# Merging w3's load into one transfer and moving it ahead of w1 at the start of an attention-plus-MLP decode kernel

## The chip, the cores and the metric

The kernel runs on one core of one Trainium2 chip. The metric is device time in microseconds (us) of one execution. All times compared here are of the fast state, unless a run is called slow. Times inside a trace are counted from the start of the span, and the span (213.7 us before) is about 1.3 us shorter than the device time of the same run.

## The reference, cut to what matters

Four sequences, one new position each. After a layer norm, an attention branch A reads 2,048 cached keys and values for each of 4 x 16 heads, and an MLP branch B runs through four weight matrices. The sum of both goes out.

```python
xn = _layernorm(x)
return x + A(xn, k_cache, v_cache, wq, wo) + B(xn, w1, w2, w3, w4)

def B(x, w1, w2, w3, w4):            # x is (4, 1, 576): S = 1
    h = _gelu(_layernorm(x) @ w1)
    # each quarter of h is shifted by one or two positions, with zeros shifted in:
    g0 = jnp.pad(h[:, :, 0*c:1*c], ((0,0),(1,0),(0,0)))[:, :S, :]      # ... g1, g2, g3 alike
    hs = jnp.concatenate([g0, g1, g2, g3], axis=-1) @ w2
    x1 = x + hs
    return x1 + _gelu(_layernorm(x1) @ w3) @ w4    # w3 is 576 x 4608
```

## The kernel before

A list of operations with keys is sorted for each engine. All large loads are issued by SyncE onto one DMA queue, in order of key: weights first, then 16 K chunks of 2 MB, then 16 V chunks (the first half of the output weights wo among them), then the rest of the output weights.

```python
ev_wq  = [add_dma([(kt_t[:], A_wq[0:512, :]...)], "wq", (), -60),
          add_dma(rag_pair(ragq3, B_w3, A_wq), "wqr", ["ragq3_zero"], -59)]   # the last 64 rows of w3 and wq
ev_r12 = add_dma(rag_pair(rag12, B_w1, B_w2), "r12", (), -58.5)
ev_w2  = add_dma([(w2main, B_w2[0:512, :]...)], "w2", (), -58)
ev_w1  = add_dma([(w1main, B_w1[0:512, :]...)], "w1", (), -57)
w3_src = B_w3[0:512, :].rearrange("(p r) n -> p r n", r=4)
ev_w3  = [add_dma([(..., w3_src[:, 2 * h:2 * h + 2, :])], ("w3", h), (), -56 + 2 * h) for h in range(2)]
ev_w3.append(ev_wq[1])
...
for c in range(NC):      # K chunks into a ring of NPOS = 4 slots: the fifth waits for PE
    add_dma(kv_pairs(A_k_cache, c), ("k", c % NPOS), [t_done(c - NPOS)] if c >= NPOS else [], c)
```

The fifth K chunk can be issued only when PE has transposed the first one. Ahead of its K loop, PE runs the front part:

```python
add("pe", pe_zero, waits=["zeros_bf", "perm_bf", "gelu_h", "x1", "xnT"], sig=None, key=-7.5)   # clears 4 banks
add("pe", pe_h(h), waits=[ev_w1, ev_r12, "xn2T", "xnT"], sig=f"hT{h}", key=-24 + 0.1 * h)      # w1's product
for n, r in enumerate((0, 1, 4, 2, 3)):                                                        # h2 = norm(x1) @ w3
    add("pe", pe_h2(r), waits=[ev_w3[r // 2]] + ([...] if r == 0 else []), ..., key=-9 + n)
...                                                                                            # GELU, 9 transposes
for c in range(NC):                                                                            # the K loop
    for k in range(NBLK):
        w = [take(("k", c % NPOS), 16)] if k == 0 else []                                      # waits for the chunk
        add("pe", pe_T(NBLK * c + k), waits=w + [...], ..., loop=lp)
```

Of the kernel before, what the change touches and what calls it, by code (L numbers as in the profile page):

```python
# [35 lines left out]
def bass_parallel_sum__sliding_block_cached__mixer_s_mlp__decode_kernel(  # L36
# [5 lines left out]
    F = B_w3.shape[1]  # L42
# [17 lines left out]
    with ExitStack() as ctx:  # L60
        def sb(name, shape, dt):
            return ctx.enter_context(nc.sbuf_tensor(name, shape, dt))
# [6 lines left out]
        w3_t = sb("w3", [128, 4 * F], BF16)  # L69
# [15 lines left out]
        w1main = w4_t[:, 0:4 * D].rearrange("p (r n) -> p r n", r=4)  # L85
# [14 lines left out]
        xnT = sb("xnT", [128, 5, 32], BF16)  # L100
        xn2T = sb("xn2T", [128, 5, B], BF16)
        x1nT = sb("x1nT", [128, 5, 32], BF16)
# [9 lines left out]
        perm_bf = sb("perm_bf", [128, 128], BF16)  # L112
# [6 lines left out]
        zeros_bf = sb("zeros_bf", [128, 512], BF16)  # L119
# [36 lines left out]
        def add(engine, emit, waits=(), sig=None, key=0.0, inc=(), loop=None, cond=None):  # L156
            seqc[0] += 1
            prog[engine].append(Op(emit, waits, sig, key, seqc[0], inc, loop, cond))

        def tok(nm):  # L160
            if nm not in S:
                S[nm] = sem("t_" + "_".join(str(k) for k in (nm if isinstance(nm, tuple) else (nm,))))
            return nm
# [6 lines left out]
        def add_dma(pairs, skey, waits=(), key=0.0, engine="sp"):  # L170
            tok(skey)
            dma_count[skey] = dma_count.get(skey, 0) + 16 * len(pairs)

            def emit(e):
                for o_, i_ in pairs:
                    e.dma_start(o_, i_).then_inc(S[skey], 16)  # L176
            add(engine, emit, waits, None, key)
            return ("dma", skey, dma_count[skey])

        def rag_pair(tile, even, odd):  # L180
            return [(tile[p:128:2, 0:w.shape[1]], w[512:576, :]) for p, w in enumerate((even, odd))]
# [8 lines left out]
        def pool_ident(t, tag, pattern, view, key):  # L190
# [20 lines left out]
            waits=["ident_f"], sig="mU", key=-8)  # L211
        for x in range(2):
# [4 lines left out]
        ev_wq = [add_dma([(kt_t[:], A_wq[0:512, :].rearrange("(p r) n -> p (r n)", r=4))], "wq", (), -60),  # L217
                 add_dma(rag_pair(ragq3, B_w3, A_wq), "wqr", ["ragq3_zero"], -59)]
        ev_r12 = add_dma(rag_pair(rag12, B_w1, B_w2), "r12", (), -58.5)
        ev_w2 = add_dma([(w2main, B_w2[0:512, :].rearrange("(p r) n -> p r n", r=4))], "w2", (), -58)  # L220
        ev_w1 = add_dma([(w1main, B_w1[0:512, :].rearrange("(p r) n -> p r n", r=4))], "w1", (), -57)
        w3_src = B_w3[0:512, :].rearrange("(p r) n -> p r n", r=4)
        ev_w3 = [add_dma([(w3_t[:, 2 * h * F:2 * (h + 1) * F].rearrange("p (r n) -> p r n", r=2), w3_src[:, 2 * h:2 * h + 2, :])], ("w3", h), (), -56 + 2 * h)
                 for h in range(2)]
        ev_w3.append(ev_wq[1])

        def kv_pairs(cache, c):
            b, gq = CH[c]
# [84 lines left out]
        for b in range(B):  # L313
            add("dve", lambda e, b=b: e.tensor_copy(out=qp_out[:, b], in_=qp_in[:, b]), waits=["qTp", "qpad_zero"],
                sig="qT" if b == B - 1 else None, key=-29.4)
# [3 lines left out]
        def pe_zero(e):  # L319
# [1 line left out]
            for q in range(4):  # L321
                ins = e.matmul(Sps[:, q, :], lhsT=zeros_bf[:, 0:128], rhs=zeros_bf[:, :], start=True, stop=True)
            return ins
        add("pe", pe_zero, waits=["zeros_bf", "perm_bf", "gelu_h", "x1", "xnT"], sig=None, key=-7.5)
        add("act", lambda e: e.activation(out=act_dummy[:], in_=zeros_bf[0:1, 0:2], func=ACTF.Sqrt), waits=["zeros_bf"], sig="sqrt_table", key=-110)
        add("act", lambda e: e.activation(out=act_dummy[:], in_=zeros_bf[0:1, 0:2], func=ACTF.Copy), waits=["zeros_bf"], inc=[(tok("evA"), 1)], key=-0.5)
        add("dve", lambda e: e.tensor_copy(out=dve_dummy[:], in_=zeros_bf[0:1, 0:2]), waits=["zeros_bf"], inc=[(tok("evD"), 1)], key=-0.5)
# [12 lines left out]
        def evac(n):  # L340
            if n % 8 in ACT_EVAC:
                return "act", lambda e: e.activation(out=ktbuf[:, n % 16], in_=tb[n % 4], func=ACTF.Copy)  # L342
            return "dve", lambda e: e.tensor_copy(out=ktbuf[:, n % 16], in_=tb[n % 4])  # L343
# [14 lines left out]
        for c in range(NC):  # L358
            lp = ("K", c // NPOS)
            for k in range(NBLK):  # L360
# [4 lines left out]
                eng, f = evac(NBLK * c + k)  # L365
                add(eng, f, waits=[f"T{NBLK * c + k}"] + ([f"SC{c - 2}"] if c >= 2 else []), inc=[("evA" if eng == "act" else "evD", 1)],
                    key=NBLK * c + k + 0.2)
# [4 lines left out]
              waits=["qT", "qs_zero"] + ([f"SC{c - NPOS}"] if c >= NPOS - 1 else []), inc=[("qs", 1)], key=c)  # L372
# [6 lines left out]
            waits=["rmax"], sig="negb", key=KS + 0.05)  # L379
        for q in range(4):  # L380
            add("act", lambda e, q=q: e.activation(out=P_sb[:, q, :], in_=Sps[:, q, :], func=ACTF.Exp,
                                                   bias=negb[:, 0:1], scale=scale, accum_out=rs4[:, q:q + 1]),
                waits=["negb"], sig=f"exp{q}", key=KS + 0.1 + 0.01 * q)

        for q in range(4):
# [3 lines left out]
                waits=[f"PTx{q}", "permT_bf"] + (["PT0"] if q == 3 else []), sig=f"PTy{q}", key=k0)  # L389
            add("act", lambda e, q=q: e.activation(out=PT_t[:, 512 * q:512 * (q + 1)], in_=ps[:, 4 + q % 3, :], func=ACTF.Copy),  # L390
                waits=[f"PTy{q}"], sig=f"PT{q}", key=k0 + 0.16)
# [3 lines left out]
            waits=["rinv", "ident_f"], sig="diag", key=KS + 0.82)  # L395
        add("pe", lambda e: e.matmul(rinvps, lhsT=ones_f[:], rhs=diag[:], start=True, stop=True), waits=["diag", "ones_f", "exp3"],
            sig="rinvp", key=KS + 0.9)
        add("dve", lambda e: e.tensor_copy(out=rinvB[:].rearrange("p (c u e) -> p c u e", u=NU, e=2),
                                           in_=rinvps.rearrange("p (u c e) -> p c u e", u=NU, e=2)),
            waits=["rinvp"], sig="rinvB", key=KS + 1.5)  # L400
# [20 lines left out]
        for c in range(NC):  # L421
# [4 lines left out]
                key=KV + 2 * c, loop=("V", gq))  # L426
            if b == B - 1:
                hv = lambda t, gq=gq: t[:, 0:128].rearrange("p (b h) -> p b h", b=B)[:, :, 8 * gq:8 * gq + 8]
                add("dve", lambda e, hv=hv: e.tensor_tensor(out=hv(OTn), in0=OTps.rearrange("p (b h) -> p b h", b=B), in1=hv(rinvB), op=ALU.mult),  # L429
                    waits=["rinvB", f"PV{c}"], sig=f"OTn{gq}" if gq == 3 else None, inc=[(tok("otn"), 1)] if gq < 3 else [], key=KV + 2 * c + 0.1)  # L430
# [13 lines left out]
        def pe_AO(half):  # L444
# [10 lines left out]
            waits=["OTy"], sig="ORp", key=KT - 2.5)  # L455
# [15 lines left out]
        def pe_h(h):  # L471
            def f(e):
                for r in range(4):
                    e.matmul(HTps[h], lhsT=xn2T[:, r, :], rhs=w1main[:, r, HALF * h:HALF * (h + 1)], start=(r == 0), stop=False)
                return e.matmul(HTps[h], lhsT=xn2T[:, 4, :], rhs=rag12[:, HALF * h:HALF * (h + 1)], start=False, stop=True)
            return f
        for h in range(2):
            add("pe", pe_h(h), waits=[ev_w1, ev_r12, "xn2T", "xnT"], sig=f"hT{h}", key=-24 + 0.1 * h)

        def pe_hs(h):  # L480
            def f(e):
# [4 lines left out]
        for h in range(2):  # L486
# [3 lines left out]
                waits=[f"hs{h}", "ln1"], sig="x1" if h else "x1a", key=-29 + 0.6 * h)  # L490
# [3 lines left out]
        add("dve", lambda e: e.tensor_copy(out=x1nT[:, :, 0:B], in_=XTps[2]), waits=["x1T", "x1nT_zero"], sig="x1nT", key=-23)  # L494
        for h in range(2):
            add("act", lambda e, h=h: e.activation(out=h_sb[:, HALF * h:HALF * (h + 1)], in_=HTps[h], func=ACTF.Gelu_apprx_tanh),
                waits=[f"hT{h}", "x1nT"], sig="gelu_h" if h else None, key=-20 + 0.1 * h)

        segs = []
        for g in range(4):  # L500
            t = 9 * g
            while t < 9 * g + 9:
                n = next(m for m, (a, z) in enumerate(W4N) if a <= t < z)
# [4 lines left out]
        def pe_h2(r):  # L508
            def f(e):
                ins = None  # L510
                for k in range(3):
                    for g, off, cnt, base_, rc, rr in sorted(segs, key=lambda x: (x[1], x[0])):
                        w, x_ = (w3r[r], x1nT[:, r, :]) if r < 4 else (ragq3, x1nT[:, 4, :])
                        ins = e.matmul(H2ps[k][32 * g:32 * g + 32, :].rearrange("p (x c) -> p x c", c=9)[:, :, off:off + cnt], lhsT=x_,
                                       rhs=w[:, base_:base_ + 128 * rc].rearrange("p (x s) -> p x s", s=rc)[:, XS[k]:XS[k + 1], rr:rr + cnt],
                                       start=(r == 0 and off == 0), stop=(r == 3), tile_position=(0, 32 * g), skip_group_check=True)
                return ins
            return f
        for n, r in enumerate((0, 1, 4, 2, 3)):
            add("pe", pe_h2(r), waits=[ev_w3[r // 2]] + (["x1nT", "qT", "qs0", "qs1"] if r == 0 else []), sig=None if r == 2 else f"h2_{r}",  # L520
                inc=[(tok("otn"), 1)] if r == 2 else [], key=-9 + n)
        for k in range(3):
            add("act", lambda e, k=k: e.activation(out=h2g[:, 9 * XS[k]:9 * XS[k + 1]], in_=H2ps[k], func=ACTF.Gelu_apprx_tanh), waits=["h2_3"],
                sig="gelu2" if k == 2 else None, key=-0.9 + 0.1 * k)

        def pe_h2T(e):
# [7 lines left out]
            waits=["h2T"], inc=[("evA", 1)], key=-0.3)  # L534
        add("dve", lambda e: e.tensor_copy(out=h2o[:, :, 8, :], in_=H2Tb.rearrange("p (g y) -> p g y", g=4)[..., 0:B]),
            waits=["h2T"], inc=[("evD", 1)], key=-0.3)
# [112 lines left out]
```

## Time and profile before

| | before |
|---|---|
| device time, median (3 runs) | 215.03 us (214.92 to 215.20) |
| bytes read from HBM | 88.49 MB |
| DMA engines busy, 12 to 176 us | 1.00 to 1.01 |
| PE ready for K / first K chunk landed | about 34 us / 35.98 us |

These are lines of the page of before. The rows with 40 digits cut the span into 40 equal slices (5.3 us each); PEclk is the TensorE clock that was granted, in tenths of full speed, and DMA the busy share of the 16 DMA engines in tenths.

```profile
span 213.7 us, 5906 instructions
...
PEclk9999999799999999999999655555555555555799
DMA  7999999999999999999999999999999999999993
GB/s 282 406 385 449 438 411 442 414 429 422 432 426 429 429 423 435 422 432 420 439 423 432 420 425 427 427 426 435 426 423 426 429 429 426 429 429 436 426 404 124
DMA packets 6690, 88.65 MB, mean 415 GB/s; under 512 B 780, under 2 KB 1048, under 8 KB 1560
...
q1 hardware_dynamic: 6664, 88.50, 97.7%
...
DMA w<-in_B_w_dram 15%; SPq L176 1%; PE ps L417 1%; PE ps L434 1%; DVE out_sb L551 0%
```

The DMA row is full from the second slice to the last but one, and the queue q1 alone has packets in flight for 97.7% of the span. The last line is the chain that ended last: it is the transfer of w4 at the end of that queue.

The table by stretches of before (start:end in us, length, busy us of each engine, granted clock, DMA share, GB/s):

```profile
core 0: us, PE busy (x) PEld busy (x) DVE busy (x) ACT busy (x) POOL busy (x), PEclk, DMA share, GB/s
12.00:18.50 6.50, 4.29 (x45) 1.68 (x45) 1.78 (x7) 0.20 (x1) 0.00 (x0) 1.00 1.01 415
18.50:24.40 5.90, 4.40 (x26) 2.24 (x23) 2.75 (x10) 0.60 (x1) 0.76 (x3) 1.00 1.00 431
24.40:30.00 5.60, 3.93 (x67) 2.60 (x69) 2.54 (x11) 2.17 (x4) 0.00 (x0) 1.00 1.00 427
30.00:36.00 6.00, 2.48 (x57) 2.04 (x49) 0.17 (x1) 1.59 (x5) 0.00 (x0) 1.00 1.01 426
36.00:114.00 78.00, 77.21 (x1274) 63.43 (x1275) 51.42 (x79) 47.14 (x47) 3.81 (x13) 0.98 1.01 427
```

In the front part, where the change works, the DMA engines are already full. PE is only partly busy, so its waits there are waits of an engine that does not set the time. In the K loop PE is busy for 77.2 of 78 us, which looks like a second bound, but the DMA engines are full there too: the two run nearly level.

PE's timeline of before around the end of the front part (start, length, instruction, and in brackets the idle time before it and what ended it):

```profile
26.61 1.51 PE L514 MATMUL ps<-w,x1nT 128*32 128x387 bf16 x36 [0.35 <-DVE x1nT L494]
28.82 0.81 PE L322 MATMUL ps<-zeros_bf 128*128 128x512 bf16 x3 [0.70 <-ACT h_sb L496]
29.56 2.17 PE L514 MATMUL ps<-w,x1nT 128*32 128x387 bf16 x54
33.07 0.76 PE L529 MATMUL ps<-ident_bf,PT 128*128 128x128 bf16 x9 [1.35 <-ACT PT L523]
36.27 2.89 PE L336 MATMUL ps<-perm_bf,ring 128*128 128x128 bf16 x32 [2.44 <-PEq L575]
```

L514 is h2, L322 the clearing of the banks, L529 the transposes of h2, L336 the K loop. PE is idle for 2.44 us ahead of the K loop; the first K chunk's semaphore is complete at 35.98 us, so this wait is for the DMA queue.

### The profile page before, as it was taken

The page shows a single profiled execution, that of the slowest core. Times are in us where ns is not written, and L with a number is a line of the kernel's source. Part 1 is how long each engine was busy: PE and PEld are TensorE (multiplying, and loading weights), DVE is VectorE, ACT ScalarE, POOL GpSimd, SP SyncE. Part 2 cuts the span into 40 slices and gives each one's busy share as a digit, 9 for nine tenths or more (in the row PEclk, how much of TensorE's full clock was granted, in tenths as well). Part 3 has the DMA queues.
Part 4 walks back from the last instruction along what each step waited for, and adds up shares of the span by engine and source line. Part 5 has one row for each costly group of instructions (what it writes and reads, how often), then busy time and mean ns, then how long its engine had stood idle before and what let it go on. Part 6 is the DMA issues. An engine that isn't in the chain of part 4 may idle for free. (4 is left out here: it accounts for less than half of the span.)

```text
span 213.7 us, 5906 instructions
## 1 busy us (share of the span) xinstructions
PE 141.4 (66%) x2664; PEld 110.4 (52%) x2668; DVE 75.3 (35%) x147; ACT 61.2 (29%) x76; POOL 10.8 (5%) x38
## 2 busy tenths in 40 slices
PE   0038683999999999999996277133444433336995
PEld 0023363788878887888774067033434433334542
DVE  0142511477776676666664830100010001001000
ACT  2001032366655666666656620000000000000000
POOL 8300100000001000000000000000000000000000
PEclk9999999799999999999999655555555555555799
DMA  7999999999999999999999999999999999999993
GB/s 282 406 385 449 438 411 442 414 429 422 432 426 429 429 423 435 422 432 420 439 423 432 420 425 427 427 426 435 426 423 426 429 429 426 429 429 436 426 404 124
DMA packets 6690, 88.65 MB, mean 415 GB/s; under 512 B 780, under 2 KB 1048, under 8 KB 1560
## 3 DMA queue, kind: packets, MB, share of 16 engines
q1 hardware_dynamic: 6664, 88.50, 97.7%
q8 instruction: 8, 0.13, 0.2%
q14 instruction: 2, 0.02, 0.0%
q10 hardware_dynamic: 16, 0.01, 0.0%
HBM read 88.49 MB, written 0.00 MB: 414 GB/s over the span
## 5 line engine op out<-in xcount | busy, mean ns | idle before, releaser
L336 PE MATMUL ps<-perm_bf,ring 128*128 128x128 bf16 x1024 | 62.5, 221 | 3.0 <-PEq L575 2.4
L336 PEld LDWEIGHTS ps<-perm_bf,ring 128*128 128x128 bf16 x1024 | 58.3, 98 | 11.3 <-issue 11.1
L343 DVE COPY kt<-ps 128x1024 bf16<-128x1024 bf16 x80 | 52.4, 688 | 28.5 <-PE ps L336 28.0
L342 ACT ACTIVATE kt<-ps 128x1024 bf16<-128x1024 bf16 x48 | 48.4, 1023 | 33.0 <-PE ps L336 32.3
L417 PE MATMUL ps<-PTpad,ring 128*128 128x8 bf16 x1024 | 29.7, 168 | 41.5 <-PEq L575 37.5
L417 PEld LDWEIGHTS ps<-PTpad,ring 128*128 128x128 bf16 x1024 | 28.7, 104 | 42.6 <-issue 42.5
L552 ACT ACTIVATE out_sb<-ps 4x288 bf16<-4x288 f32 x1 | 0.4, 401 | 87.5 <-PE ps L434 87.5
L350 PE MATMUL ps<-kt,Qs 128*32 128x512 bf16 x272 | 18.5, 393 | 1.4 <-PEq L575 1.4
L406 DVE TENSOR_TENSOR PTpad<-PT,mU_bf 128x512 bf16<-128x512 bf16 x16 | 6.4, 421 | 29.7 <-PE ps L417 29.7
L429 DVE TENSOR_TENSOR OTn<-ps,rinvB 128x32 bf16<-128x32 f32 x4 | 0.8, 192 | 34.5 <-PE ps L417 34.5
L277 PE MATMUL ps<-ident_bf,xn_bf 4*128 4x4 bf16 x8 | 0.5, 170 | 13.9 <-DVE ragsrc L271 13.9
L350 PEld LDWEIGHTS ps<-kt,Qs 128*32 128x32 bf16 x272 | 5.9, 98 | 7.2 <-issue 2.2
L371 POOL COPY Qs<-Qpad 128x128 bf16<-128x128 bf16 x16 | 4.6, 293 | 86.8 <-PE ps L350 72.5
L277 PEld LDWEIGHTS ps<-ident_bf,xn_bf 4*128 4x128 bf16 x8 | 0.4, 111 | 14.0 <-issue 11.6
L434 PE MATMUL ps<-w,ORT 128*4 128x288 bf16 x64 | 5.8, 358 | 0.4 <-DVE ORT L456 0.4
L551 DVE CAST out_sb<-ps 4x288 bf16<-4x288 f32 x1 | 0.4, 446 | 14.5 <-PE ps L434 14.5
L434 PE MATMUL ps<-w,h2T_sb 128*4 128x288 bf16 x72 | 5.0, 286 | 0.4 <-DMA w<-in_B_w_dram 0.4
L264 ACT ACTIVATE sd<-mv 4x1 f32<-4x1 f32 x3 | 0.6, 202 | 15.8 <-DVE mv L262 15.8
L388 PE MATMUL ps<-kt,permT_bf 128*128 128x512 bf16 x3 | 1.8, 608 | 4.9 <-DVE kt L387 4.8
L434 PEld LDWEIGHTS ps<-w,ORT 128*4 128x4 bf16 x64 | 3.4, 106 | 3.0 <-DVE ORT L456 1.0
L434 PEld LDWEIGHTS ps<-w,h2T_sb 128*4 128x4 bf16 x72 | 2.9, 84 | 2.8 <-DMA w<-in_B_w_dram 1.8
L440 PE MATMUL ps<-zeros_bf 128*128 128x512 bf16 x13 | 3.8, 419 | 0.4 <-DVE OTn L429 0.2
(99 smaller groups left out, 65.9 us busy)
## 6 DMA issues: line engine op xcount, KB each, us to landing
ring<-in_A_k_cache_dram SPq DMA_DIRECT2D x16, 2048.0 KB, 14.4
ring<-in_A_v_cache_dram SPq DMA_DIRECT2D x16, 2048.0 KB, 17.4
w<-in_B_w_dram SPq DMA_DIRECT2D x2, 2304.0 KB, 21.9
w<-in_A_wo_dram SPq DMA_DIRECT2D x2, 2304.0 KB, 21.1
kt<-in_A_wq_dram SPq DMA_DIRECT2D x1, 4096.0 KB, 12.3
w<-in_B_w_dram SPq DMA_DIRECT2D x1, 2592.0 KB, 28.1
w<-in_B_w_dram SPq DMA_DIRECT2D x3, 576.0 KB, 13.6
w<-in_B_w_dram SPq DMA_DIRECT2D x1, 1296.0 KB, 30.7
```

What stands on the lines that cost most here:

```text
L277: e.transpose(XTps[idx][:, r, :], v[:, r, :], ident_bf[0:B, 0:B])
L336: ins = e.transpose(tb[n % 4][:, t, :], slot_t(c)[:, 8 * k + t, :], perm_bf[:])
L342: return "act", lambda e: e.activation(out=ktbuf[:, n % 16], in_=tb[n % 4], func=ACTF.Copy)
L343: return "dve", lambda e: e.tensor_copy(out=ktbuf[:, n % 16], in_=tb[n % 4])
L350: ins = e.matmul(Sps[32 * u:32 * u + 32, q, :].rearrange("p (t i) -> p t i", t=16), lhsT=Qs[:, c % NPOS, 32 * u:32 * u + 32], rhs=ktgrp[:, ...
L371: P(lambda e, c=c, cc=cc: e.tensor_copy(out=Qs[:, c % NPOS, :], in_=Qpad_t[:, 128 * cc:128 * cc + 128]), waits=["qT", "qs_zero"] + ([f"SC{ ...
L388: add("pe", lambda e, q=q: e.matmul(ps[:, 4 + q % 3, :], lhsT=permT_bf[:], rhs=PTx[:, q, :], start=True, stop=True), waits=[f"PTx{q}", "pe ...
L406: return lambda e: e.tensor_tensor(out=PTpad[:, c % 2], in0=PTv[:, :, cc, :].unsqueeze(2).to_broadcast([128, NT, NU, 2]), in1=mU_bf[:].uns ...
L417: ins = e.matmul(o_, lhsT=slot_t(c)[:, t, :], rhs=PTpad[:, c % 2, t].rearrange("p u e -> p (u e)"), start=(t == 0), stop=(t == NT - 1))
L429: add("dve", lambda e, hv=hv: e.tensor_tensor(out=hv(OTn), in0=OTps.rearrange("p (b h) -> p b h", b=B), in1=hv(rinvB), op=ALU.mult), waits ...
L434: return e.matmul(ACC[h], lhsT=lhsT, rhs=rhs, start=start, stop=stop, tile_position=(0, 32 * h), skip_group_check=True)
L440: ins = e.matmul(ps[:, 3, :], lhsT=zeros_bf[:, 0:128], rhs=zeros_bf[:, :], start=True, stop=True)
```

## The change

The intent: w3's 512 main rows come as one transfer, in one run of 36,864 B per partition in place of two of 18,432 B, and earlier; w1, whose result is needed later, comes behind it, and PE multiplies with w1 after h2.

```diff
-        ev_w1 = add_dma([(w1main, B_w1[0:512, :].rearrange("(p r) n -> p r n", r=4))], "w1", (), -57)
-        w3_src = B_w3[0:512, :].rearrange("(p r) n -> p r n", r=4)
-        ev_w3 = [add_dma([(..., w3_src[:, 2 * h:2 * h + 2, :])], ("w3", h), (), -56 + 2 * h) for h in range(2)]
-        ev_w3.append(ev_wq[1])
+        ev_w3 = add_dma([(w3_t[:], B_w3[0:512, :].rearrange("(p r) n -> p (r n)", r=4))], "w3", (), -57)
+        ev_w1 = add_dma([(w1main, B_w1[0:512, :].rearrange("(p r) n -> p r n", r=4))], "w1", (), -56)
...
-        add("pe", pe_zero, ..., key=-7.5)
+        add("pe", pe_zero, ..., key=-0.5)
...
-            add("pe", pe_h(h), waits=[ev_w1, ev_r12, "xn2T", "xnT"], sig=f"hT{h}", key=-24 + 0.1 * h)
+            add("pe", pe_h(h), waits=[ev_w1, ev_r12, "xn2T", "xnT"], sig=f"hT{h}", key=-3 + 0.1 * h)
...   (the GELU of h moves from key -20 to -0.69, behind that of h2)
-        for n, r in enumerate((0, 1, 4, 2, 3)):
-            add("pe", pe_h2(r), waits=[ev_w3[r // 2]] + (["x1nT", "qT", "qs0", "qs1"] if r == 0 else []), ...
+        for n, r in enumerate((4, 0, 1, 2, 3)):
+            add("pe", pe_h2(r), waits=["x1nT", "qT", "qs0", "qs1", ev_wq[1]] if r == 4 else [ev_w3], ...
```

(The accumulation's `start` flag moves with the order, from r == 0 to r == 4, the ragged 64 rows.)

More of the change, by code (lines that the diff above doesn't have):

```diff
@@ L220, in bass_parallel_sum__sliding_block_cached__mixer_s_mlp__decode_kernel @@
         ev_w2 = add_dma([(w2main, B_w2[0:512, :].rearrange("(p r) n -> p r n", r=4))], "w2", (), -58)
-        ev_w1 = add_dma([(w1main, B_w1[0:512, :].rearrange("(p r) n -> p r n", r=4))], "w1", (), -57)
-        w3_src = B_w3[0:512, :].rearrange("(p r) n -> p r n", r=4)
-        ev_w3 = [add_dma([(w3_t[:, 2 * h * F:2 * (h + 1) * F].rearrange("p (r n) -> p r n", r=2), w3_src[:, 2 * h:2 * h + 2, :])], ("w3", h), (), -56 + 2 * h)
-                 for h in range(2)]
-        ev_w3.append(ev_wq[1])
+        ev_w3 = add_dma([(w3_t[:], B_w3[0:512, :].rearrange("(p r) n -> p (r n)", r=4))], "w3", (), -57)
+        ev_w1 = add_dma([(w1main, B_w1[0:512, :].rearrange("(p r) n -> p r n", r=4))], "w1", (), -56)
         def kv_pairs(cache, c):
@@ L323, in pe_zero @@
             return ins
-        add("pe", pe_zero, waits=["zeros_bf", "perm_bf", "gelu_h", "x1", "xnT"], sig=None, key=-7.5)
+        add("pe", pe_zero, waits=["zeros_bf", "perm_bf", "gelu_h", "x1", "xnT"], sig=None, key=-0.5)
         add("act", lambda e: e.activation(out=act_dummy[:], in_=zeros_bf[0:1, 0:2], func=ACTF.Sqrt), waits=["zeros_bf"], sig="sqrt_table", key=-110)
@@ L496, in bass_parallel_sum__sliding_block_cached__mixer_s_mlp__decode_kernel @@
             add("act", lambda e, h=h: e.activation(out=h_sb[:, HALF * h:HALF * (h + 1)], in_=HTps[h], func=ACTF.Gelu_apprx_tanh),
-                waits=[f"hT{h}", "x1nT"], sig="gelu_h" if h else None, key=-20 + 0.1 * h)
+                waits=[f"hT{h}", "x1nT"], sig="gelu_h" if h else None, key=-0.69 + 0.01 * h)
         segs = []
@@ L515, in f @@
                                        rhs=w[:, base_:base_ + 128 * rc].rearrange("p (x s) -> p x s", s=rc)[:, XS[k]:XS[k + 1], rr:rr + cnt],
-                                       start=(r == 0 and off == 0), stop=(r == 3), tile_position=(0, 32 * g), skip_group_check=True)
+                                       start=(r == 4 and off == 0), stop=(r == 3), tile_position=(0, 32 * g), skip_group_check=True)
                 return ins
             return f
-        for n, r in enumerate((0, 1, 4, 2, 3)):
-            add("pe", pe_h2(r), waits=[ev_w3[r // 2]] + (["x1nT", "qT", "qs0", "qs1"] if r == 0 else []), sig=None if r == 2 else f"h2_{r}",
+        for n, r in enumerate((4, 0, 1, 2, 3)):
+            add("pe", pe_h2(r), waits=["x1nT", "qT", "qs0", "qs1", ev_wq[1]] if r == 4 else [ev_w3], sig=None if r == 2 else f"h2_{r}",
                 inc=[(tok("otn"), 1)] if r == 2 else [], key=-9 + n)
```

## The prediction

> **What bounds the kernel now.** The DMA queue. The stretch table gives a DMA share of 1.00 to 1.01 in every stretch from 12 to 176 us, at 415 to 431 GB/s; the queue table gives that queue 97.7% of the span. The idle time is the start (first packet ends about 3 us in) and the tail (last landing about 211.5 us, span 213.7 us). The chain of waits ends with 32.3 us of W4 transfer. The Trainium skill, "DMA: Bandwidth & Descriptors", section "Where 436 GB/s comes from", puts the fabric ceiling at 435 GB/s; this trace, at up to 431 GB/s, agrees. Only fewer bytes, better packets, or an idle gap can change the time.
>
> **What the change does to DMA.** Same bytes, same order up to w2, then w3 before w1. 256 packets of 18,432 B (median 686 ns each, 26.9 B/ns per engine) become 128 of 36,864 B. The packet records give 309 ns for 8,192 B and 1,222 ns for 32,768 B: about 5 ns per packet that does not scale with bytes (estimate from these two). An engine saves 8 packets, so about 0.04 us. One issue of 0.44 us leaves SyncE, which runs far ahead. Value: nothing.
>
> **What it does to PE and ACT.** Landings before (DMA semaphore records): w2 17.5, w1 18.9, w3 24.4 and 29.9, first K chunk 36.0 us. After: w3 whole at about 28.5, w1 at 29.9, first K chunk unchanged at 36.0. The layer-norm path gives x1nT at 26.5 us. h2 now does the ragged rows at 26.6 to 27.4, waits for w3 until about 28.5, then runs 72 matmuls at about 41 ns each (timeline: 54 in 2.17 us), so it ends at about 31.6 us, against 31.7 us before. The first half's early work was never the bound: the second half landed at 29.9. After it: GELU 1.3 us on ACT, with its 1.28 us table load already moved ahead of the wait (instruction order), w1's product 1.2 us on PE under it, 9 transposes 0.8 us, the second GELU 0.7 us, the zeroing matmuls about 0.8 us, now last. PE is ready for K at about 34.7 to 35 us; the first K chunk lands at 36.0, and the timeline of before shows PE idle 2.44 us for it. Roughly 1 us of slack is left; if it were overrun, PE takes about 4.7 us per K chunk against 4.9 us of transfer, and the ring's fifth issue (42.7 us) comes 8 us before the fourth chunk lands (50.7 us). None of this is on the critical path.
>
> **Predicted time: 215.0 us, 80% range 214.5 to 215.6 us. Faster by over 2%: 0.005; within 2%: 0.98; slower by over 2%: 0.015.**
>
> **What would show it.** Right: the first K chunk lands at 36.0 ± 0.2 us; PE's idle before its first transpose is still ended by that landing; 128 packets of 36,864 B at about 1,370 ns; DMA share about 1.0 from 12 to 176 us; last W4 landing about 211.5 us. h2 ends 31 to 32 us.
>
> **What would make it wrong.** The 36 KB run being cut into many short packets with a lower rate (no packet in the trace exceeds 32,768 B): 1,152 B packets run at 22.6 B/ns, which would cost w3 about 2 us. Or one DMA engine lagging through the long packets so all later landings wait on it. Or PE's wait on w3 growing past the K slack and the ring's slack together, over 8 us.

## More of the kernel before

With S = 1 every shift by one position leaves zeros only, so `hs` is zero and `h` reaches no output. The kernel before uses the zeros (`hs_inT` is a memset) but still loads w1 and w2 and runs their products.

## The result, and the profile after

| | before | after |
|---|---|---|
| device time, median (6 runs each) | 215.06 us (214.81 to 215.25) | 214.90 us (214.80 to 215.03) |
| ratio after / before | | 0.9994, 95% interval 0.9981 to 1.0007 |

A ratio here is the mean time of one kernel's fast runs over that of the other's fast runs of the same rounds, so it is not quite the ratio of the medians quoted. The time is the same.

The same lines of the page of after:

```profile
span 213.6 us, 5903 instructions
...
PEclk9999959999999999999999555555555555555799
DMA  7999989999999999999999999999999999999993
...
DMA packets 6546, 88.65 MB, mean 415 GB/s; under 512 B 764, under 2 KB 1032, under 8 KB 1544
...
q1 hardware_dynamic: 6520, 88.50, 97.8%
...
DMA w<-in_B_w_dram 15%; SPq L176 1%; PE ps L414 1%; PE ps L431 1%; DVE out_sb L548 0%
```

There are 144 packets fewer (128 of data, and 16 that add to a semaphore), the bytes and the queue's share are the same, and the chain ends in the same transfer. In the front part one digit of PEclk is new: a 5 in the sixth slice, where h2 runs. The 7 that before has in its eighth slice, at the start of the K loop, is gone.

The table by stretches of after:

```profile
12.00:18.50 6.50, 4.70 (x45) 1.63 (x45) 1.35 (x5) 0.77 (x2) 0.00 (x0) 1.00 1.10 461
18.50:24.40 5.90, 3.52 (x18) 1.87 (x18) 2.87 (x13) 0.62 (x3) 0.77 (x3) 1.00 0.94 406
24.40:30.00 5.60, 2.78 (x48) 2.06 (x49) 1.85 (x8) 0.90 (x1) 0.00 (x0) 0.65 0.93 395
30.00:36.00 6.00, 5.56 (x72) 4.18 (x69) 0.17 (x1) 2.17 (x7) 0.00 (x0) 0.76 1.01 431
36.00:114.00 78.00, 76.68 (x1272) 62.24 (x1271) 51.09 (x79) 47.66 (x47) 3.85 (x13) 1.00 1.01 427
```

The DMA shares 1.10, 0.94 and 0.93 are no idle time: packets of 1.36 us blur the edges of such short stretches. Weighted by their lengths the first three rows give 0.99. What did change is PE: its granted clock is 0.65 and 0.76 in two stretches, against 1.00 before.

PE's timeline of after (line numbers are three lower than before; L471 is w1's product, in its new place):

```profile
25.50 0.98 PE L511 MATMUL ps<-w,x1nT 128*32 128x387 bf16 x18 [0.26 <-DVE x1nT L491]
28.51 4.70 PE L511 MATMUL ps<-w,x1nT 128*32 128x387 bf16 x69 [2.04 <-DMA w<-in_B_w_dram]
...
33.61 0.65 PE L471 MATMUL ps<-w,xn2T 128*4 128x288 bf16 x4
...
34.77 0.77 PE L526 MATMUL ps<-ident_bf,PT 128*128 128x128 bf16 x9 [0.39 <-ACT PT L520]
35.59 0.81 PE L319 MATMUL ps<-zeros_bf 128*128 128x512 bf16 x3
36.36 1.95 PE L333 MATMUL ps<-perm_bf,ring 128*128 128x128 bf16 x32
```

h2 waits 2.04 us for the whole of w3, then takes 4.70 us for 69 of its matmuls, where the predicted rate gave 2.8 us. The idle time ahead of the K loop is gone, and yet the K loop starts at 36.36 us in place of 36.27 us. (x itself landed at 8.27 us in this trace against 9.30 us before. The landing of x varies between 8.0 and 9.3 us over all traces, so PE's front part starts up to 1 us earlier or later whatever the kernel.)

When each transfer was complete, from the records of the DMA semaphores (us; where two numbers stand, the first and the last of its 16 engines):

| | w2 | w1 | w3 | first K chunk | last piece of w4 |
|---|---|---|---|---|---|
| before | 16.91 / 17.52 | 18.34 / 18.94 | 23.84 / 24.44, then 29.33 / 29.93 | 34.21 / 35.98 | 211.48 |
| after | 17.05 / 17.53 | 29.42 / 29.90 | 27.97 / 28.47 | 34.31 / 36.01 | 211.38 |

By first engines, w3 took 29.33 - 18.34 = 10.99 us before and 27.97 - 17.05 = 10.92 us after. All else is an exchange of places, and from the first K chunk on the queue is the same.

### The profile page after: what moved, and what is told of

Read it like the earlier page. It is cut to its first block, busy times and chain, and to the rows that moved or that the text cites. A ratio compares the mean times of both kernels' runs of the same rounds, so it can differ in the third digit from the quotient of the medians.

```text
span 213.6 us, 5903 instructions
## 1 busy us (share of the span) xinstructions
PE 142.3 (67%) x2664; PEld 110.4 (52%) x2668; DVE 75.2 (35%) x147; ACT 61.8 (29%) x76; POOL 10.9 (5%) x38
## 5 line engine op out<-in xcount | busy, mean ns | idle before, releaser
L333 PEld LDWEIGHTS ps<-perm_bf,ring 128*128 128x128 bf16 x1024 | 57.5, 98 | 10.7 <-issue 10.7
L339 ACT ACTIVATE kt<-ps 128x1024 bf16<-128x1024 bf16 x48 | 49.2, 1024 | 30.8 <-PE ps L333 29.5
L347 PE MATMUL ps<-kt,Qs 128*32 128x512 bf16 x272 | 17.8, 382 | 1.4 <-PEq L572 1.4
L511 PE MATMUL ps<-w,x1nT 128*32 128x387 bf16 (+7 forms) x90 | 5.9, 404 | 2.3 <-DMA w<-in_B_w_dram 2.0
L511 PEld LDWEIGHTS ps<-w,x1nT 128*32 128x32 bf16 x90 | 4.5, 124 | 3.6 <-DMA w<-in_B_w_dram 2.3
```

The costliest lines, as they stand in the source:

```text
L333: ins = e.transpose(tb[n % 4][:, t, :], slot_t(c)[:, 8 * k + t, :], perm_bf[:])
L339: return "act", lambda e: e.activation(out=ktbuf[:, n % 16], in_=tb[n % 4], func=ACTF.Copy)
L347: ins = e.matmul(Sps[32 * u:32 * u + 32, q, :].rearrange("p (t i) -> p t i", t=16), lhsT=Qs[:, c % NPOS, 32 * u:32 * u + 32], rhs=ktgrp[:, ...
L511: ins = e.matmul(H2ps[k][32 * g:32 * g + 32, :].rearrange("p (x c) -> p x c", c=9)[:, :, off:off + cnt], lhsT=x_, rhs=w[:, base_:base_ + 1 ...
```

## The experiments

Theory: the DMA queue's bytes set the time; the change moves no bytes, and the front part of PE is hidden. Rivals: the time hangs on when PE is ready for K; or long runs have a gain of their own that a late PE took back. Each run was timed five or six times beside the kernel before on the same chip (median of before 215.12 us for the first four, 214.98 us for the next four, 215.04 us for the last two). One execution of before beside the second four was slow (229.02 us, mean clock 0.68) and is left out of the ratios. All outputs were correct.

### One w3 transfer alone

```diff
 (kernel before)
-        ev_w3 = [add_dma(... two halves ...)]
+        ev_w3 = [add_dma([(w3_t[:], B_w3[0:512, :].rearrange("(p r) n -> p (r n)", r=4))], "w3", (), -56)] * 2
```

> The kernel before with one part of the change alone: w3 as one transfer in 36 KB runs, still behind w1, PE's order untouched. Theory (the DMA queue's bytes set the time): ratio 0.998 to 1.002; w3 lands whole at 29.9 us, h2's first product waits for it, h2 ends at 33 to 35 us (36 us or later if the clock is granted at half), PE is late for the first K chunk by up to 2 us, and the time does not move. Rival (the time hangs on when PE is ready for K): 1 to 2 us slower, ratio 1.005 to 1.009.

Measured: 215.14 us, ratio 1.0002 (0.9988 to 1.0015). PE's timeline of this run:

```profile
30.09 2.74 PE L512 MATMUL ps<-w,x1nT 128*32 128x387 bf16 x36 [4.93 <-DMA w<-in_B_w_dram]
...
34.58 2.67 PE L512 MATMUL ps<-w,x1nT 128*32 128x387 bf16 x54
...
39.37 1.95 PE L334 MATMUL ps<-perm_bf,ring 128*128 128x128 bf16 x32
```

PE waits 4.93 us for w3 and starts the K loop at 39.37 us, 3.1 us later than before. That is more than the 2 us expected, because the clock was granted at half from 25.4 to 35.7 us; h2 ended at 37.3 us. The time does not move. This alone refutes the first rival: three microseconds of PE's readiness cost nothing.

### The new order alone

```diff
 (kernel after)
-        ev_w3 = add_dma([(w3_t[:], ...)], "w3", (), -57)
+        ev_w3 = [add_dma([(..., w3_src[:, 2 * h:2 * h + 2, :])], ("w3", h), (), -57 + 0.1 * h) for h in range(2)]
```

> The changed kernel with w3 in two transfers of 18 KB runs again, so that only the order (w3 ahead of w1, w1's product behind h2) is left of the change. Theory: ratio 0.998 to 1.002 against the kernel before; w3 lands at 23.0 and 28.5 us, h2 starts on the first half at about 26 us. PE waits less, so the clock stays granted longer than in the changed kernel and h2 ends near 31.5 us. Rival: the 36 KB runs carry a gain of their own, then this is slower than the changed kernel by more than 0.2 us.

Measured: 215.16 us, ratio 1.0003 (0.9989 to 1.0016). Both parts alone are the same as before, and so are both together. The second half of w3 was complete at 30.08 us, not 28.5: its last engine came 2.0 us after its first (28.04), which the expectation did not have. The clock did not stay granted longer than in after either: it was at half in two pieces, 24.38 to 27.79 and 31.20 to 34.61 us, and h2 ended at about 31.9 us. This run was not slower than after by more than the intervals can tell (they reach 0.3 us either way), so a gain of the long runs alone, if there is one, is below that.

### w1 taken away

```diff
 (kernel after)
-        ev_w1 = add_dma(...)
-        for h in range(2):
-            add("pe", pe_h(h), ...)                  # and the GELU of h, and the waits on them
```

> The changed kernel without w1's main transfer (0.59 MB) and without its product and GELU, whose result nothing uses (with one position, the shifts replace all of h by zeros). Theory (bytes in the queue set the time): 1.38 us less (0.59 MB at 427 GB/s), ratio 0.993 to 0.995, first K chunk lands at 34.6 us. Rival (time hangs on PE's work, or on runs and order): within 0.3 us of before, or a gain that differs from 1.38 us by over 0.5 us.

Measured: 213.50 us, ratio 0.9926 (0.9913 to 0.9940), which is 1.6 us less. The expected 1.38 us (ratio 0.9936) lies inside the interval. The first K chunk was complete at 34.50 us in place of 36.01 us. Taking 0.59 MB out of the queue does at once what exchanging 5.3 MB within it could not.

### w3 in 1,152-byte runs

```diff
 (kernel after)
+        ev_w3 = [add_dma([(w3_dst[:, :, D*j:D*(j+1)], w3_src[:, :, D*j:D*(j+1)])], "w3", (), -57 + 0.01 * j) for j in range(8)][-1]
```

> The changed kernel with w3 cut into 8 column transfers of 1,152-byte runs: 4,096 packets for w3 in place of 128, same bytes, same place in the queue. Theory: each packet costs 51 ns (measured for that size in the profile of before) against 1,364 ns for 32 of them in one run, so 8 x (32 x 51 - 1,364) ns = 2.1 us more per DMA engine, all of it in the time: ratio 1.008 to 1.012, first K chunk at about 38.1 us. Rival (a later w3 is hidden in the ring's slack, or run length hardly matters at all): ratio below 1.004.

Measured: 216.27 us, ratio 1.0055 (1.0041 to 1.0069), 1.2 us more. Run length counts, and what it costs in the front part goes into the time in full, but the size was half of what was expected. The expectation multiplied the packet's recorded duration (51 ns). By first engines, w3 took 29.18 - 17.07 = 12.11 us here against 10.92 us in after: 1.19 us for 248 more packets on each engine, or 4.8 ns per packet. The recorded durations of short packets overlap, as the DMA share of 1.10 in the stretch from 17.5 to 30.5 us of this run also says. The 4.8 ns agree with the prediction's estimate of about 5 ns per packet. (The edit also makes eight transfers of one, and no run separates the two, so the 4.8 ns hold both.) At that price, the 8 packets that the change saves on each engine are worth 0.04 us.

### PE made late on purpose: 4 and 12 us

```diff
 (kernel after, pe_zero)
-            for q in range(4):
+            for q in [0, 1, 2, 3] * 6:        # * 15 for the second run
                 ins = e.matmul(Sps[:, q, :], lhsT=zeros_bf..., rhs=zeros_bf..., start=True, stop=True)
```

> The changed kernel with 20 more zeroing matmuls (216 ns each at full clock, 4.3 us) on PE just ahead of the K loop. Theory (DMA queue sets the time; the ring of four K chunks has about 7 us of slack at its fifth issue): PE starts the K loop at about 40.7 us, 4 us after the first chunk has landed, the fifth K issue moves from 41.7 to about 46 us, and the time stays: ratio 0.998 to 1.003. Rival (PE's readiness sets the time): 4 us slower, ratio 1.018.

> The same with 56 more zeroing matmuls (12.1 us at full clock). Theory: this overruns the slack. The fifth K issue moves to about 54 us, after the fourth chunk has landed (50.9 us), the DMA engines run dry for some 5 us, and the time grows by about 4 to 6 us, not by 12: ratio 1.018 to 1.028. Rival (PE's readiness counts in full): ratio 1.055. If the DMA queue could not run dry at all: ratio 1.000.

Measured, 4 us: median 215.06 us, ratio 1.0040 (0.9997 to 1.0083). Four of six runs lie between 214.85 and 215.06 us, two at 216.94 and 217.64 us. The profiled run (214.92 us) starts its K loop at 39.76 us and issues the fifth K chunk at 44.61 us. In the profiled run the lateness is hidden, but the mean lies above the expected 1.003, and the two longer runs say that this kernel stands near an edge.

Measured, 12 us: 223.14 us, ratio 1.0389 (1.0371 to 1.0406), 8.2 us more, above the 4 to 6 us expected. The table by stretches of this run:

```profile
48.00:52.00 4.00, 4.00 (x67) 3.14 (x66) 1.98 (x3) 1.32 (x2) 0.29 (x1) 1.00 0.15 57
52.00:56.00 4.00, 4.00 (x72) 3.24 (x69) 3.27 (x5) 2.67 (x3) 0.12 (x1) 1.00 0.46 160
56.00:60.00 4.00, 4.00 (x75) 3.65 (x76) 2.89 (x5) 2.96 (x3) 0.17 (x1) 1.00 1.01 412
60.00:64.00 4.00, 4.00 (x76) 3.58 (x64) 2.59 (x5) 2.61 (x3) 0.29 (x1) 1.00 0.99 385
64.00:68.00 4.00, 4.00 (x72) 3.24 (x70) 2.79 (x5) 2.28 (x3) 0.29 (x1) 1.00 1.03 360
```

The DMA share falls to 0.15 and 0.46: the queue ran dry. The fifth issue came at 53.04 us, its first packets at 54.37 us, while the first engine had finished the fourth chunk at 48.90 us, so there were 5.5 us without work. Then the rate stays below 427 GB/s for some stretches, with at most two transfers in the queue: the first engine of the eighth K chunk lands 6.9 us later than in after. The last engine falls behind by about a further 1.1 us (the end of w4 is 8.0 us later). The expectation had only the first of these three terms.

### PE's gaps filled

```diff
 (kernel after)
+        add("pe", pe_fill(2, 10), waits=["zeros_bf"], sig=None, key=-23.5)   # 10 dummy matmuls ahead of x1's transposes
+        add("pe", pe_fill(2, 9), waits=["zeros_bf"], sig=None, key=-8.5)     # 9 between the ragged rows and w3
```

> The changed kernel with 19 dummy matmuls in the two gaps in which PE idled there (10 at 22.2 to 24.9 us, 9 at 26.5 to 28.5 us). Theory of h2's stretch (4.7 us in the changed kernel against the predicted 2.95): PE's granted clock fell to a half after the gaps; with the gaps filled it stays at 1.0, h2 takes about 3.0 us after w3's landing and ends at about 31.6 us, PE is idle again for 1 us or more ahead of the first K chunk, and the time stays: ratio 0.998 to 1.002. Rival for the stretch (w3's data or the matmuls' order slows them): h2 still takes over 4 us at full clock.

Measured: 214.99 us, ratio 0.9998 (0.9985 to 1.0011). PE's timeline of this run:

```profile
29.21 2.61 PE L520 MATMUL ps<-w,x1nT 128*32 128x387 bf16 x69
...
36.18 1.95 PE L342 MATMUL ps<-perm_bf,ring 128*128 128x128 bf16 x32 [1.16 <-PEq L581]
```

The granted clock stays at 1.0 from 23 to 118 us. The same 69 matmuls of h2 take 2.61 us in place of 4.70 us, and 1.16 us of idle time ahead of the K loop are back. h2's stretch was the clock, not w3's data or the matmuls' order; and the device time does not care.

### All dead work taken away

```diff
 (kernel after, without w1 as above)
-        ev_r12 = add_dma(rag_pair(rag12, B_w1, B_w2), "r12", (), -58.5)
-        ev_w2 = add_dma(...)
-        (w2's product and the two additions of it)
+        add("dve", lambda e: e.tensor_copy(out=x1_bf[:], in_=xn_bf[:]), waits=["ln1"], sig="x1", key=-29)
```

> The changed kernel without w1, w2, their ragged rows, and the products that use them (with one position the shifted groups are all zero, so hs is zero and x1 is the normed x): 1.33 MB less. Theory: 3.1 to 3.3 us less (w1 1.43, w2 1.43, ragged rows 0.38 us of landings in the changed kernel), ratio 0.984 to 0.987, faster than both kernels. Rival (PE's readiness for K sets the time once the chunk lands 3 us earlier): a gain of under 2 us.

Measured: 211.84 us, ratio 0.9851 (0.9838 to 0.9864), 3.2 us less, as expected. The output is correct, because `hs` is zero for one position. With the run without w1 (1.6 us less), this is one of the two versions here that beat both kernels, and both do so through fewer bytes in the queue, 1.33 MB here. It holds for S = 1 only, as the kernel before already does.

### The same lateness in both kernels

Did the change use up slack? Both kernels got 36 more zeroing matmuls just ahead of their K loop.

```diff
 (kernel after)   for q in [0, 1, 2, 3] * 10:
 (kernel before)  add("pe", pe_late, waits=["zeros_bf"], sig=None, key=-0.5)      # 36 such matmuls
```

> The changed kernel with 36 more zeroing matmuls (7.8 us at full clock) ahead of the K loop. Theory, mended by the run with 12 us: what counts is when the fifth K issue comes. It moves from 41.7 to about 49.3 us, its first packets start 1.3 us later, at 50.6 us, and 15 of the 16 DMA engines have run dry at 48.9 us: 1.7 us of dry queue and up to 1.5 us of slower chunks after it, ratio 1.007 to 1.016. Rival (the cost of lateness begins at once, 8 of 12 us of the earlier dose): ratio 1.025 or more. If the ring still hides it: 1.000.

> The kernel before with the same 36 matmuls just ahead of its K loop. There PE was idle from about 33.9 to 36.3 us, an idle time that the changed kernel no longer has. If the change has used up that slack, the same dose makes the K loop start at about 42.1 us here against 44.5 us in the changed kernel, the fifth K issue comes at about 46.9 us, its packets at 48.2 us, just ahead of the dry queue (48.9 us), and the time stays: ratio 0.998 to 1.004, at least 1 us below the changed kernel with the same dose. Rival (the change left the slack as it was): both doses cost the same within 0.3 us.

Measured in fast runs: after with the dose, median 222.37 us (220.89 to 223.54), ratio 1.0351 (1.0313 to 1.0389); before with the dose, median 217.97 us (217.22 to 218.45), ratio 1.0133 (1.0114 to 1.0151). One run of each (224.37 and 221.20 us) is called slow only because it lies over 1.5% above the fastest of its kernel; its mean clock (0.793 and 0.798) is no lower than that of fast runs. Both cost more than expected, and the expectation that before would hide the dose was wrong. The comparison stands: the same dose costs after some 4.7 us more (0.0218 of 215 us; 4.1 us with the two runs called slow). PE's timelines, after with the dose first, then before with the dose:

```profile
35.07 8.80 PE L319 MATMUL ps<-zeros_bf 128*128 128x512 bf16 x40
46.09 1.95 PE L333 MATMUL ps<-perm_bf,ring 128*128 128x128 bf16 x32 [2.22 <-PEq L572]
```

```profile
34.62 7.93 PE L327 MATMUL ps<-zeros_bf 128*128 128x512 bf16 x36
43.06 1.95 PE L342 MATMUL ps<-perm_bf,ring 128*128 128x128 bf16 x32 [0.51 <-PEq L581]
```

In these two traces the K loop starts 3.0 us apart. The zeroing ends at about 43.9 us in the first and 42.5 us in the second: 1.3 us of the difference are PE's longer front part, so some slack was used up, though less than the 2.4 us expected. (In this trace of before with the dose, the second half of w3 was complete only at 31.13 us, against 29.93 us in the trace of before, and the transposes of h2 started 1.0 us later than there.) A further 1.7 us come from a gap between the zeroing and the K loop, 2.22 us against 0.51 us, although the first K chunk has long landed. The trace shows where PE's sequencer was: at the branch that opens the K loop (L605 of the first kernel, L614 of the second; count, shortest, median and longest in ns, first and last start in us):

```profile
L605 PEldq COMPARE_BRANCH  x10: 76/210/5838, 39.9 to 201.2; - x10
L614 PEldq COMPARE_BRANCH  x10: 76/210/4127, 38.6 to 198.1; - x10
```

This opening branch is the longest of each line, 5.84 and 4.13 us, against 0.32 to 0.40 us in the other ten traces. It ended at 45.77 and 42.75 us, in both about 1.4 us after the end of a 16 KB transfer of the instruction queue (43.32 to 44.42 us and 40.29 to 41.39 us). That fits a PE that waited for its own next instructions, which more zeroing matmuls ahead of the loop may have brought about; no run separates it. The profiled run of after with the dose (221.26 us) is one of the quicker of its five fast runs; the slower ones left no trace to look at.

The profiled runs together, in order of the fifth K issue:

| run | K loop starts | fifth K issue | time over median of before |
|---|---|---|---|
| after | 36.36 | 41.20 | -0.1 |
| before | 36.27 | 42.71 | 0 |
| one w3 transfer alone | 39.37 | 44.22 | 0.0 |
| after, 4 us late | 39.76 | 44.61 | -0.1 |
| before, 8 us late | 43.06 | 47.91 | 2.9 |
| after, 8 us late | 46.09 | 50.94 | 6.2 |
| after, 12 us late | 48.19 | 53.04 | 8.1 |

(All in us. The 41.7 us of the expectations is the end of after's fifth issue; its start, as in the other rows, is 41.20 us.) In these traces lateness is free up to 44.6 us; the last three rows cost about the issue time minus 45 us. The edge of 45 us is read off these three rows; no traced run lies between 44.61 and 47.91 us. The first engine runs out of work at 48.9 us, so by this reading the issue has to come about 4 us ahead of that. Of these, 1.3 us are issue to first packet. Why the rest is needed is only partly shown, by the low rates after a dry queue. The two longer runs of the 4 us dose would fit a fifth issue 2 to 3 us later in them, but they left no trace.

## Why the prediction was right, point by point

- **The bound.** Right, and shown: bytes taken out of the queue come out of the time (1.6 us for 0.59 MB, 3.2 us for 1.33 MB), and 3.1 us of lateness of PE does not go in.
- **Nothing from long runs.** Right. 128 packets of 36,864 B at 1,364 ns (predicted about 1,370); w3's stretch shrank by 0.07 us. The estimate of 5 ns per packet agrees with the 4.8 ns measured. The Trainium skill, page "DMA: Bandwidth & Descriptors", section "Rules for kernel authors", asks for at least 1 MiB per DMA; the two halves of w3, 2.36 MB each, were past that and ran at up to 431 GB/s already.
- **The landings.** Right: first K chunk 36.01 us (36.0 predicted), w3 28.47 (28.5), w1 29.90 (29.9), last w4 211.38 (211.5).
- **The table load moves ahead of the wait.** Right: it runs at 24.02 us, during the wait.
- **h2's length.** Wrong in size. The prediction took "72 matmuls at about 41 ns each" and an end at 31.6 us. h2 ended at about 33.4 us, with 69 matmuls in 4.70 us, 68 ns each. The term that failed is the clock: w1's product no longer filled PE's gap, so PE waited 2.7 us and then 2.0 us, and the granted clock was a half from 26.06 to 32.89 us. With both gaps filled the same 69 matmuls took 2.61 us at full clock. The clock fell before the second wait began (26.5 us), so by this trace the first wait started it; no run fills one gap alone. Nor is w1's product in its old place enough: with one w3 transfer alone it ran there, at 22.8 to 24.2 us, and the clock fell at 25.43 us all the same.
- **The slack.** "Roughly 1 us" ahead of the K loop became none, so the prediction's check that this idle time "is still ended by that landing" failed too. The second term that failed is the ring: the prediction named "over 8 us" for both slacks together, and the runs put the edge near a fifth issue at 45 us, 3.8 us later than after's 41.20 us.

So the time was right for the stated reason, but the margin behind it was less than half of what was claimed. The edge of 45 us is 2.3 us beyond before's fifth issue and 3.8 us beyond after's. After's is the earlier one because before starts its K loop at half clock (37.05 to 40.46 us), after that 2.44 us idle time. Yet with the same dose ahead of the K loop, after ends 4.7 us behind, of which only 1.3 us of PE's own work are shown; another 1.7 us passed at the branch that opens the K loop, and the rest is open.

## What to carry to other kernels

Where one DMA queue is full from end to end, the order of its transfers and the length of runs that were long already were worth nothing here; ask which bytes could stay in HBM. Before a wait is moved onto an engine with slack, count the engine's clock as well as its instructions: two gaps of 2 to 3 us were enough to halve the rate of what followed. The slack of this ring ended about 4 us before the queue was empty, so measure it by adding lateness rather than by subtracting times in one trace.

## What the Trainium skill lacked or had wrong

- "DMA: Bandwidth & Descriptors", section "Where 436 GB/s comes from": read alone, this passage says that for transfers from HBM to SBUF the HBM side, about 358 GB/s, binds. Here the kernel's one core held 427 GB/s for 78 us of 2 MB transfers, well above that. The page has the missing condition elsewhere, in the note under its table of measurements: about 358 GB/s is the rate of each core when both cores of an HBM domain stream.
- The same page, "Why small descriptors are slow (HBM only)": it gives a fixed cost per packet of about 3 cycles and a 256 B example. It gives this in cycles, not in time. In these runs 1,152 B packets cost 4.8 ns each over long ones (with w3 in eight transfers in place of one), and the recorded packet durations overlap (DMA share 1.10), so that the durations overstate the cost by nearly a factor of two (2.1 us expected, 1.2 us measured).
- "TensorE: Matmul & The Clock Gate", "Part 1: The HAM clock gate (the "warmup" mystery)": it says that the clock halves after an idle window of about 3.4 us, in free-running windows. The halved stretches in the front parts here are 3.41, 6.83 and 10.24 us long, which agrees. But a window need not be idle: PE was busy for 0.88 us of the 3.41 us before the drop in after, and 0.97 us before the drop in before. Busy time alone does not settle it: a window with 1.50 us busy kept the full clock (before with the dose, 29.37 to 32.78 us), and one with 1.81 us busy lost it (one w3 transfer alone, 22.02 to 25.43 us). The page names no such share.
- None of the pages read here says how early the next transfer has to be issued to keep a queue full. Here it was about 4 us ahead of the first engine's last packet, by the edge of 45 us.
- None of them tells of this: in all twelve traces, every transfer is complete on its 16 engines within 0.8 us until the first 16 KB transfer of the instruction queue in the front part (at 27 to 34 us). With the next one or two transfers the last engine is 1.4 to 2.1 us behind the first, and it stays at least 1.4 us behind to the end (before: the last piece of w4 at 209.34 us on its first engine, 211.48 us on its last). No run here takes the instruction transfers away, so the cause is open.
